# First q pieces on the ACT queue, and a split last eviction, in a two-layer attention kernel

## The chip, the cores and the metric

The kernel runs on one core of a Trainium2 chip. The metric is the device time of one execution in microseconds (us). The profile is that of one execution, taken by the hardware profiler. Engines are PE (matrix multiply), PEld (its weight loads, which overlap it), DVE, ACT, POOL and SP. SP computes nothing here: it issues the transfers (DMAs) between HBM and the on-chip memory SBUF. PE writes its results to PSUM, which has eight banks, and DVE or ACT copy them to SBUF ("eviction").

## The reference

```python
def _attn_ref(q, k, v):                      # batch 4, 12 heads, seq 448, head_dim 64
    scores = q @ k.T / sqrt(64), causal mask, softmax (eps 1e-9)
    return attn @ v
def _moe_ref(x, w_gate, wq, wk, wv, wo):     # x: 4 x 448 x 768, 4 experts, 2 chosen per token
    w = softmax over the two largest of x @ w_gate
    for e in range(4):                       # each expert is one causal attention head of width 64
        ye = causal_attention(x @ wq[e], x @ wk[e], x @ wv[e]) @ wo[e]
        out += (token chose e) * w_e * ye
    return out                               # 4 x 448 x 768
```

The output of the first layer, with its heads side by side, is the `x` of the second.

## The kernel before

The first layer works on 24 pairs of heads (four batches of six). A pair's k and q come as one tile `raw` of 128 partitions (two heads of 64) by 2 by 448 floats; index 0 of the middle dimension is k, index 1 is q. For each pair PE makes the scores in four row blocks (L362, in the order 1, 0, 2, 3), DVE subtracts the mask and takes the row maximum (L371), ACT takes the exponential (L378), POOL or ACT scales by the inverse sum, PE transposes (L407), DVE or ACT evicts, and PE multiplies with v (L422). The second layer of a batch projects x to queries and keys (L491) and to values and gates (L528), runs the same attention for two pairs of experts, and multiplies by `wo` in `output` (L594).

Nothing runs in the order in which it is written. Each step is put on record by `add(rank, kind, {engine: cost}, emit, after, bufs)`, and a planner (`Plan.run`) goes through an estimated time in which PE, ACT, DVE, POOL and "DMA" each do one step at a time: the ready step of the lowest rank starts. After that loop has ended, the line `for _, op, e in order: op.emit(e)` calls the recorded functions, in the order of their planned starts, and this writes the instructions of all queues. A step becomes ready 0.22 us after one on PE that it needs, and 0.2 us after one on another compute engine (FROM_PE, FROM_REST). The framework below adds the semaphores that the data need; each engine and each issuing queue then runs its instructions strictly in order.

The very first pair is loaded in four pieces (L449 to L454): the rows of k and q for columns 0 to 223, then those for columns 224 to 447, each 128 rows of 896 bytes, all issued by SP. Score blocks 1 and 0 need the first two pieces, blocks 2 and 3 all four. SP goes on with v of that pair (L470) and with whole tiles of the next pairs (L461).

`output(rank, b)` has a loop over m = 0 to 5, the 128-row parts of the output of batch b. Each has a PSUM bank (kind "pj", at most three at once; banks go back to a stock of eight and the one longest free is taken next). In the last batch the PE work of an m is two steps of three matmuls: pair 0, then pair 1. Then an eviction "ob" of 128x448 (ACT 0.43 or DVE 0.54 by the planner) goes into a half of the SBUF tile `ob`, and a store "st" (1.2 by the planner) from SP writes 128 rows of 1792 bytes to `out[b, m]` in HBM. In the other batches one store takes two m.

Of the kernel before, what the change touches and what calls it, by code (L numbers as in the profile page):

```python
# [17 lines left out]
def f32(ap):  # L18
    return ap.bitcast(F32)
# [24 lines left out]
class Plan:  # L44
# [16 lines left out]
    def add(self, rank, kind, on, emit, after=(), bufs=()):  # L61
        op = Op(rank, kind, on, emit, after, bufs)
        op.n = len(self.ops)
        self.ops.append(op)
        return op
# [122 lines left out]
def tile_attention_then_moe_attention(  # L188
# [27 lines left out]
    nc = tc.nc  # L216
    B, NM, _, S = out.shape
    NP = v.shape[1]
    P = 128
# [4 lines left out]
    DM = NM * P  # L224
# [64 lines left out]
    add = plan.add  # L289
# [9 lines left out]
    MOVE = {"ACT": 0.43, "DVE": 0.54}  # L299

    def copy(e, out, in_):
        if e == "ACT":
            nc.scalar.activation(out, in_, AF.Copy)  # L303
        else:
            nc.vector.tensor_copy(out, in_)  # L305
# [7 lines left out]
    def sub(e, out, a, b):  # L313
        eng = nc.gpsimd if e == "POOL" else nc.vector
        eng.tensor_tensor(out=out, in0=a, in1=b, op=ALU.subtract)  # L315
# [122 lines left out]
    def first_layer(b, p):  # L438
        rank = float(b * NP + p)
        raw, vt, hb, lb = Buf("raw"), Buf("v"), Buf("hi"), Buf("lo")  # L440
        first = (b, p) == pairs[0]
        full = b * NP + p in FULL
        cuts = (0, 2 * C, S) if first else (0, S)
        ready = []
        vl = None
        for lo, hi in zip(cuts, cuts[1:]):
            at = slice(lo, hi)
            part = (hi - lo) / S
            if first:  # L449
                loads = [  # L450
                    add(rank - 2.5, "ld", {"DMA": 0.6},
                        lambda e, n=n, at=at: nc.sync.dma_start(raw.at[:, n, at], qk[b, p, :, n, at]), (), [raw])
                    for n in range(2)
                ]  # L454
                hs = loads if full else [
                    add(rank + 0, "hi", {("DVE", "ACT")[n]: 0.32},
                        lambda e, n=n, at=at: copy(e, hb.at[:, n, at], raw.at[:, n, at]), [loads[n]], [raw, hb])
                    for n in range(2)
                ]
            else:  # L460
                loads = [add(rank - 2.5, "ld", {"DMA": 2.4}, lambda e: nc.sync.dma_start(raw.at, qk[b, p]), (), [raw])]  # L461
                hs = 2 * loads if full else 2 * [add(rank + 0, "hi", {"ACT": 0.85, "DVE": 0.54}, lambda e: copy(e, hb.at, raw.at), loads, [raw, hb])]
            ready += hs
            ready += hs if full else [
                add(rank - 1.5, "lo", {"POOL": 1.1 * part},
                    lambda e, n=n, at=at: sub(e, lb.at[:, n, at], raw.at[:, n, at], f32(hb.at)[:, n, at]), [hs[n]],
                    [raw, hb, lb])
                for n in range(2)
            ]
        vl = add(rank - 1.5, "ld", {"DMA": 1.2}, lambda e: nc.sync.dma_start(vt.at, v[b, p]), (), [vt])  # L470
        dest = xbuf[b, p] = Buf("x")
        xdone[b, p] = attention(
            rank, "a", b, p, [raw] if full else [hb, lb], ready, lambda h, j: vt.at[:, h * NC + j], [vl, vt], None, dest
        )

    def second_layer(b):
# [32 lines left out]
        for p in range(2):  # L509
# [3 lines left out]
                lambda h, j, p=p: vb.at[:, j, 2 * p + h], [vdone, vb], (gt, gdone), dest,  # L513
            )
        output(rank + 4, b)

    def values(rank, b, vb, gt, big):
# [63 lines left out]
    def output(rank, b):  # L581
        for m in range(DM // P):
            cols = slice(m * P, m * P + P)
            ps = Buf("pj")
            prev = None
            if m % 2 == 0:
                ob = Buf("osb")
                moved = []
            for ks in ((0,), (1,)) if b == B - 1 else ((0, 1),):

                def mm(e, ks=ks, ps=ps, cols=cols):
                    for p in ks:
                        for n, (w, t) in enumerate(((woh, 0), (woh, 1), (wol, 0))):
                            nc.tensor.matmul(  # L594
                                ps.at[:, :S], w[:, p, cols], ubuf[b, p].at[:, t],
                                start=(p == 0 and n == 0), stop=(p == 1 and n == 2),
                            )

                after = [udone[b, p] for p in ks] + [split[6 + p] for p in ks] + [prev]
                prev = add(rank, "pjo", {"PE": 0.62 * len(ks)}, mm, after, [ps] + [ubuf[b, p] for p in ks])  # L600
            moved.append(add(
                rank, "ob", MOVE,
                lambda e, m=m, ps=ps, ob=ob: copy(e, ob.at[:, m % 2], ps.at[:, :S]), [prev], [ps, ob],
            ))
            if b == B - 1:
                add(rank, "st", {"DMA": 1.2}, lambda e, m=m, ob=ob: nc.sync.dma_start(out[b, m], ob.at[:, m % 2]),
                    moved[-1:], [ob])
            elif m % 2:
                add(rank, "st", {"DMA": 2.4},
                    lambda e, m=m, ob=ob: nc.sync.dma_start(  # L610
                        out[b, m - 1:m + 1].rearrange("m p s -> p m s"), ob.at), moved, [ob])
# [18 lines left out]
    for b, p in pairs:  # L630
        first_layer(b, p)
# [43 lines left out]
```

## Time and profile before

| what | us |
|---|---|
| median of three runs | 331.93 |
| the runs | 331.35, 331.93, 1099.09 |
| the profiled execution | 331.19 |
| its span, first to last instruction | 329.4 |
| PE busy in it | 320.3 (97%) |
| ACT, DVE, POOL busy | 238.3, 214.7, 160.7 |
| DMA queue of SP, share of 16 DMA engines | 24.0% |

The span is what the views of the trace show; 1.8 us of the execution lie outside it. A busy share is a mean over stages that differ, so the views by stage are read beside it. A timeline row gives the start, the length, the engine, the source line, the operation, the tiles written and read, and in brackets the idle time before it with what ended it.

### The profile page before, as it was taken

Reading aid. Unit: us, or ns where it says so; the run is one execution under the profiler, and the core shown is the slowest. Engines: PE = TensorE matmul, PEld = TensorE weight load, DVE = VectorE, ACT = ScalarE, POOL = GpSimd, SP = SyncE. Lnnn points to the kernel's source line nnn. Section 1 sums busy time; section 2 is a strip of 40 time slices with the busy share of each in tenths; the row PEclk is TensorE's granted clock in tenths of the full one; section 3 lists DMA queues with packets and bytes.
Section 4 is the critical chain, followed back from the end, with each engine's and each line's share of the span. In section 5 each row is a group of like instructions: output and inputs, shape, how many; then the busy total and the mean of one; then the engine's idle time right before and its main releaser. Section 6 shows DMA issues by size and latency. Waiting matters only on the chain.

```text
span 329.4 us, 7473 instructions
## 1 busy us (share of the span) xinstructions
PE 320.3 (97%) x2584; PEld 259.5 (79%) x2584; DVE 214.7 (65%) x785; ACT 238.3 (72%) x743; POOL 160.7 (49%) x273
## 2 busy tenths in 40 slices
PE   5899999999999999999999999999999999999995
PEld 3467677778968977879799778887799978988784
DVE  2889789879688596466854599727672464544730
ACT  4999797779887699576875699948694464616833
POOL 2586989888985425909454136917421102001100
PEclk9999999999999999999999999999999999999999
DMA  5762563443362000163120010121000000000124
GB/s 167 248 192 87 158 201 125 132 111 100 103 194 90 2 30 29 57 203 135 56 63 22 2 50 10 30 102 67 2 2 3 0 0 2 1 2 0 58 111 167
DMA packets 11461, 25.65 MB, mean 78 GB/s; under 512 B 1184, under 2 KB 4768, under 8 KB 11424
## 3 DMA queue, kind: packets, MB, share of 16 engines
q1 hardware_dynamic: 11424, 25.18, 24.0%
q8 instruction: 20, 0.33, 0.4%
q14 instruction: 17, 0.14, 0.1%
HBM read 19.67 MB, written 5.51 MB: 76 GB/s over the span
## 4 chain that ended last, share of the span: by engine, by line
PE 62%; POOL 0%; ACT 0%; issue 0%
PE ps L491 14%; PE ps L422 12%; PE ps L407 11%; PE ps L594 9%; PE ps L362 9%; PE ps L528 8%; POOL five L311 0%; ACT raw L303 0%
## 5 line engine op out<-in xcount | busy, mean ns | idle before, releaser
L311 POOL TENSOR_SCALAR five<-five,stat 112x112 f32<-112x112 f32 (+3 forms) x218 | 105.5, 505 | 105.4 <-DVE stat L389 65.4
L378 ACT ACTIVATE five<-five,stat 112x336 f32<-112x336 f32 (+3 forms) x256 | 131.8, 518 | 14.6 <-DVE stat L371 14.5
L371 DVE CUSTOM_DVE_ANT_0 five<-ps,mask 112x224 f32<-112x224 f32 (+3 forms) x256 | 99.0, 442 | 31.1 <-PE ps L362 30.4
L407 PE MATMUL ps<-ident,five 112*112 112x112 f32 x640 | 70.6, 261 | 1.0 <-POOL five L311 0.5
L407 PEld LDWEIGHTS ps<-ident,five 112*112 112x112 f32 x640 | 63.4, 133 | 8.3 <-POOL five L311 2.2
L315 POOL TENSOR_TENSOR two<-raw,two 128x448 fp32r<-128x448 f32 x34 | 38.6, 1153 | 43.4 <-DVE two L305 10.7
L491 PE MATMUL ps<-two,wqkh 128*128 128x448 f32 x192 | 57.0, 377 | 0.4 <-DVE two L315 0.2
L303 ACT ACTIVATE five<-ps 112x448 f32<-112x448 f32 x92 | 46.5, 540 | 11.7 <-PE ps L407 11.0
L305 DVE COPY five<-ps 112x448 f32<-112x448 f32 x68 | 40.9, 620 | 20.7 <-PE ps L407 19.5
L422 PE MATMUL ps<-five,v 112*64 112x448 f32 (+3 forms) x384 | 50.3, 404 | 0.0
L378 ACT ACTIVATION_READ_ACCUMULATOR five<-five,stat 112x1 f32 x256 | 48.5, 189 | 0.0
L422 PEld LDWEIGHTS ps<-five,v 112*64 112x64 f32 x384 | 25.4, 137 | 23.6 <-issue 11.8
L362 PE MATMUL ps<-two,two 64*112 64x448 f32 (+3 forms) x400 | 41.7, 299 | 0.0
L491 PEld LDWEIGHTS ps<-two,wqkh 128*128 128x128 f32 x192 | 34.3, 188 | 4.4 <-issue 0.8
L315 DVE TENSOR_TENSOR two<-ps,two 128x448 fp32r<-128x448 f32 x48 | 29.9, 622 | 11.8 <-ACT two L303 10.8
L528 PE MATMUL ps<-wvh,two 128*112 128x260 f32 x192 | 35.7, 287 | 0.0
L491 PE MATMUL ps<-two,wqkl 128*128 128x448 f32 x96 | 35.1, 366 | 0.0
L362 PE MATMUL ps<-two 64*112 64x224 f32 (+3 forms) x200 | 33.3, 326 | 0.0
L362 PEld LDWEIGHTS ps<-two,two 64*112 64x112 f32 x400 | 31.4, 172 | 1.1 <-issue 0.2
L303 ACT ACTIVATE two<-ps 128x448 fp32r<-128x448 f32 x23 | 12.5, 543 | 24.4 <-PE ps L491 16.3
L528 PEld LDWEIGHTS ps<-wvh,two 128*112 128x112 f32 x192 | 28.0, 175 | 1.1 <-DVE stat L371 0.6
L594 PE MATMUL ps<-two,woh 128*128 128x448 f32 x96 | 28.1, 374 | 0.0
(55 smaller groups left out, 322.2 us busy)
## 6 DMA issues: line engine op xcount, KB each, us to landing
raw<-in_qk_dram SPq DMA_DIRECT2D x23, 448.0 KB, 3.6
v<-in_v_dram SPq DMA_DIRECT2D x24, 224.0 KB, 2.6
out_dram<-raw SPq DMA_DIRECT2D x9, 448.0 KB, 2.6
raw<-in_wqk_dram SPq DMA_DIRECT2D x4, 384.0 KB, 3.5
out_dram<-raw SPq DMA_DIRECT2D x6, 224.0 KB, 1.9
raw<-in_wvg_dram SPq DMA_DIRECT2D x2, 390.0 KB, 3.2
raw<-in_wo_dram SPq DMA_DIRECT2D x2, 384.0 KB, 3.0
raw<-in_qk_dram SPq DMA_DIRECT2D x4, 112.0 KB, 2.2
```

The costliest lines, as they stand in the source:

```text
L303: nc.scalar.activation(out, in_, AF.Copy)
L305: nc.vector.tensor_copy(out, in_)
L311: (nc.gpsimd if e == "POOL" else nc.vector).tensor_scalar(t, t, r, 1.0, op0=ALU.mult, op1=ALU.mult)
L315: eng.tensor_tensor(out=out, in0=a, in1=b, op=ALU.subtract)
L362: nc.tensor.matmul(banks[h].at[:C, :m], ops[x].at[sides[h], 1, qc], ops[y].at[sides[h], 0, :m], start=(n == 0), stop=(n == len(terms) - 1),)
L371: lambda e, h=h, i=i, m=m, bank=banks[h]: nc.vector.tensor_tensor_reduce(out=w(h, i), in0=bank.at[:C, :m], in1=mask[:, S - m:], scale=-0.1 ...
L378: lambda e, h=h, i=i: nc.scalar.activation(w(h, i), w(h, i), AF.Exp, bias=stat.at[:, 0, h, i:i + 1], scale=-1.0, accum_out=stat.at[:, 1, h ...
L407: nc.tensor.transpose(bank.at[:C, at * C:at * C + C], w(h, i)[:, j * C:j * C + C], ident[:C, :C])
L422: nc.tensor.matmul(acc.at[sides[h], j * C:S], vals(h, j), pt.at[:, bank, at:at + S - j * C], start=(j == 0), stop=(j == NC - 1),)
L491: nc.tensor.matmul(ps.at[:, :S], w[:, 2 * sel + p, k], xbuf[b, k].at[:, t], start=(k == 0 and n == 0), stop=(k == NP - 1 and n == 2),)
L528: nc.tensor.matmul(ps.at[:C, :VC], xbuf[b, k].at[:, t, c * C:c * C + C], w[:, k], start=(k == 0 and n == 0), stop=(k == NP - 1 and n == 2),)
L594: nc.tensor.matmul(ps.at[:, :S], w[:, p, cols], ubuf[b, p].at[:, t], start=(p == 0 and n == 0), stop=(p == 1 and n == 2),)
```

## The change

Two edits. In `first_layer`, the two q pieces of the first pair are issued by ACT, the two k pieces still by SP. In `output`, the eviction step gets a function `move`: where the flag `last` is true, ACT copies columns 0 to 223 and issues a store of them, and DVE copies columns 224 to 447 and SP issues a store of those; where it is false, the chosen engine copies all 448 columns. For the last m of the last batch the step is planned on ACT alone, and its store step is not added.

```diff
-                        lambda e, n=n, at=at: nc.sync.dma_start(raw.at[:, n, at], qk[b, p, :, n, at]), (), [raw])
+                        lambda e, n=n, at=at: (nc.sync, nc.scalar)[n].dma_start(raw.at[:, n, at], qk[b, p, :, n, at]), (), [raw])
...
-            moved.append(add(
-                rank, "ob", MOVE,
-                lambda e, m=m, ps=ps, ob=ob: copy(e, ob.at[:, m % 2], ps.at[:, :S]), [prev], [ps, ob],
-            ))
-            if b == B - 1:
+            last = b == B - 1 and m == DM // P - 1
+
+            def move(e, m=m, ps=ps, ob=ob):
+                for x, n in (("ACT", 0), ("DVE", 1)) if last else ((e, slice(None)),):
+                    n = slice(n * S // 2, (n + 1) * S // 2) if last else n
+                    copy(x, ob.at[:, m % 2, n], ps.at[:, :S][:, n])
+                    if last:
+                        (nc.scalar if x == "ACT" else nc.sync).dma_start(out[b, m, :, n], ob.at[:, m % 2, n])
+
+            moved.append(add(rank, "ob", {"ACT": 0.43} if last else MOVE, move, [prev], [ps, ob]))
+            if last:
+                pass
+            elif b == B - 1:
                 add(rank, "st", {"DMA": 1.2}, lambda e, m=m, ob=ob: nc.sync.dma_start(out[b, m], ob.at[:, m % 2]),
                     moved[-1:], [ob])
```

## Rows read from the trace of the kernel before

**Rows 1.** Busy time by stage, core 0, us from the start; columns as the head says.
```profile
core 0: us, PE busy (x) PEld busy (x) DVE busy (x) ACT busy (x) POOL busy (x), PEclk, DMA share, GB/s
0.00:3.50 3.50, 0.00 (x0) 0.00 (x0) 0.00 (x0) 1.28 (x1) 2.22 (x13) 1.00 0.43 104
3.50:5.40 1.90, 1.46 (x8) 1.16 (x8) 0.60 (x3) 0.17 (x1) 0.00 (x0) 1.00 0.92 234
5.40:12.00 6.60, 5.76 (x26) 3.06 (x26) 4.56 (x28) 6.05 (x24) 1.33 (x4) 1.00 0.61 195
12.00:20.00 8.00, 7.66 (x54) 4.65 (x56) 7.77 (x40) 7.97 (x29) 6.30 (x13) 1.00 0.69 229
20.00:100.00 80.00, 79.64 (x708) 61.45 (x705) 68.18 (x235) 68.81 (x225) 69.81 (x103) 1.00 0.47 141
100.00:300.00 200.00, 199.94 (x1622) 167.85 (x1621) 122.92 (x457) 138.90 (x430) 79.41 (x139) 1.00 0.12 38
```

**Rows 2.** The chain of waits, its end: start, length, what.
```profile
318.41 7.42 PE ps L594 x36
325.83 0.02 issue
325.86 0.54 ACT raw L303
```

**Rows 3.** Timeline, the first 6 us.
```profile
0.79 1.28 ACT L378 ACT_TABLE_LOAD   x1 [0.79 <-PEq L664]
0.80 1.80 SPq L452 DMA_DIRECT2D raw<-in_qk_dram  x4
2.64 0.43 SPq L470 DMA_DIRECT2D v<-in_v_dram  x1
3.58 1.46 PE L362 MATMUL ps<-raw 64*112 64x224 f32 x8 [3.58 <-DMA raw<-in_qk_dram]
...
5.23 0.48 ACT L378 ACTIVATE five<-five,stat 112x224 f32<-112x224 f32 x1 [3.15 <-DVE stat L371]
...
5.43 3.12 PE L362 MATMUL ps<-raw 64*112 64x336 f32 x14 [0.39 <-DMA raw<-in_qk_dram]
```

**Rows 4.** Line 452, the four piece loads: issue ns, then landing us (min/median/max).
```profile
L452 SPq DMA_DIRECT2D raw<-in_qk_dram x4: 372/422/432, 0.8 to 2.2; - x4
DMA to landing us min/median/max: 2.0/2.2/3.1
```

**Rows 5.** Two stretches: piece loads of 896-byte rows, stores of 1792-byte rows.
```profile
2.40:2.90 0.50, 0.00 (x0) 0.00 (x0) 0.00 (x0) 0.00 (x0) 0.50 (x4) 1.00 0.92 224
322.60:323.90 1.30, 1.30 (x9) 1.21 (x8) 0.00 (x0) 0.64 (x2) 0.00 (x0) 1.00 1.02 376
```

**Rows 6.** Timeline, the last evictions and stores.
```profile
321.05 1.74 ACT L303 ACTIVATE raw<-ps 128x448 f32<-128x448 f32 x3 [2.05 <-PE ps L594]
...
321.62 5.14 SPq L606 DMA_DIRECT2D out_dram<-raw  x6
...
323.45 0.54 ACT L303 ACTIVATE raw<-ps 128x448 f32<-128x448 f32 x1 [0.66 <-PE ps L594]
...
324.65 0.54 ACT L303 ACTIVATE raw<-ps 128x448 f32<-128x448 f32 x1 [0.66 <-PE ps L594]
...
325.86 0.54 ACT L303 ACTIVATE raw<-ps 128x448 f32<-128x448 f32 x1 [0.66 <-PE ps L594]
```

**Rows 7.** The sixth and last store's issue; then line 606, issue ns and landing us.
```profile
326.43 0.33 SPq L606 DMA_DIRECT2D out_dram<-raw  x1
...
L606 SPq DMA_DIRECT2D out_dram<-raw x6: 332/332/350, 321.6 to 326.4; - x6
...
DMA to landing us min/median/max: 1.9/1.9/2.0
```

**Rows 8.** DMA from 318 to 330 us in 40 slices of 0.3 us: GB/s.
```profile
GB/s 382 382 376 257 0 0 0 0 0 0 0 0 0 0 42 364 364 370 364 371 376 42 42 370 347 6 42 370 347 6 42 370 341 12 0 0 0 0 0 0
```

**Rows 9.** Copies out of PSUM by shape: busy us, mean ns of one, idle before.
```profile
L303 ACT ACTIVATE raw<-ps 128x448 f32<-128x448 f32 x20 | 10.9, 544 | 12.0 <-PE ps L594 11.6 <-issue 0.3
L305 DVE COPY vb<-ps 112x256 f32<-112x256 f32 x8 | 3.3, 423 | 4.0 <-PE ps L528 2.5 <-PE ps L422 1.3
L303 ACT ACTIVATE vb<-ps 112x256 f32<-112x256 f32 x8 | 3.1, 384 | 14.8 <-PE ps L528 10.9 <-PE ps L422 3.9
L305 DVE COPY raw<-ps 128x448 f32<-128x448 f32 x4 | 2.5, 624 | 2.3 <-POOL two L315 1.3 <-PE ps L594 0.9
```

**Rows 10.** Timelines of ACT and DVE: two copies of one PSUM bank.
```profile
248.04 0.39 ACT L303 ACTIVATE vb<-ps 112x256 f32<-112x256 f32 x1 [0.99 <-PE ps L528]
...
248.46 0.16 DVE L305 COPY gate<-ps 112x4 f32<-112x4 f32 x1 [2.07 <-ACT vb L303]
```

## Prediction

> **What bounds the kernel.** I read the busy time by stage first. From 20 us on, PE is busy 79.64 of 80 us and then 199.94 of 200 [rows 1]: no other engine's speed counts there. What PE does not fill lies at the two ends, and both edits are there. At the start PE waits 3.58 us for the first k and q pieces and 0.39 us more, at 5.43, for the other two [rows 3]; between 5.4 and 20 us it loses 0.84 and 0.34 us to ACT and DVE, ACT being busy 7.97 of 8 us [rows 1]. These follow the first scores, so what PE gains before 5.43 moves the rest with it. At the end the chain of waits reads PE until 325.83, one 0.54 us eviction on ACT, the end [rows 2]; then the last store is issued at 326.43 and lands 1.9 us later, at 328.33 [rows 7], 1.07 us before the span ends.
>
> **What the second edit really does.** The function `move` takes `m`, `ps` and `ob` as default arguments, but reads `last` from the loop around it. It is called when the planner has finished, long after the loop over m; by then `last` holds the value of m = 5. For batches 0 to 2 that is false, for the last batch it is true for all six m. The `if last: pass` branch, however, runs inside the loop and drops the store step of m = 5 only. So all six evictions of the last batch are split and store two halves each, and m = 0 to 4 are stored again whole. The stores go from 6 to 17, their bytes from 6 to 11 units of 229,376 B (224 KB), and five DRAM blocks are written twice.
>
> **Costs at the start.** SP issues a piece in 372 to 432 ns [rows 4], so q's first piece leaves at about 1.23 now and at 0.80 when ACT issues it. ACT is free: its only early work is the table load at 0.79, which carries the line of the first exponential, stands behind the two issues in its queue and, ending near 2.9, still precedes the first exponential at 5.23 [rows 3]. No row has a DMA issued by ACT; I price it as SP's, 0.33 to 0.43 us [rows 4, 7]. The gain is at most 0.43 us by issue. By transport: two pieces, 229,376 B, at the 224 GB/s of [rows 5] take 1.02 us, which is 0.51 more than one; the first piece, issued at 0.80, lands at 2.80 [rows 3, 4], so both by about 3.3, 0.3 before PE's 3.55. The 0.39 us wait for the second pieces is governed by one that takes 3.1 us to land [rows 4]; it is issued some 0.95 us earlier, but v and the next tile leave SP 0.9 us earlier too and compete. If it lands no sooner, PE gains nothing at all; if sooner, up to 0.4 + 0.39. A longer issue on ACT could cost 0.3. I take a gain of 0.35, range +0.8 to -0.3.
>
> **Costs at the end.** PE's own work is unchanged, 325.83 still (less the gain): banks are read until at most 323.35 for m = 2 below, while m = 5 starts at 324.65, so no matmul waits for a bank.
>
> A half copy on ACT: from 384 ns at 256 columns and 544 at 448 [rows 9], 0.83 ns a column, hence 0.36 us. On DVE, 423 and 624 give 0.39 us. The halves do not run together: a DVE copy of four columns from a bank that ACT reads sits idle 2.07 us and starts 0.03 us after ACT's copy ends [rows 10]. That both only read, and different columns, is what the Trainium skill ("PSUM — Partial Sum Buffer", section "PSUM bank collisions raise a hardware error") adds: two engines may not be in one bank of the same partitions at once, reads included. Side by side a split would be done 0.39 us after PE, in sequence after 0.78; that is 0.24 later than the 0.54 of now, with the row deciding.
>
> For m = 0 then: ACT 321.05 to 321.41, its store issued at 321.43, DVE to 321.83, SP's half store h0 at 321.86. ACT's issue holds up its next copy until 321.81 (m = 1 is ready at 321.65 [rows 6]); h1 follows at 322.61. Behind DVE nothing is queued. What matters is SP. A whole store f0 writes bytes that two half stores in flight are writing; I expect it to be held until these have landed, and everything behind it in SP's queue with it. The order is that of planned starts: counted from PE's end of m = 0, the evictions start at 0.22, 0.84, 1.46, 2.70, 3.94, 5.18, the whole stores at 0.85 (0.22 + 0.43 + 0.2) and then 1.2 apart. So SP has h0 h1 f0 h2 f1 h3 f2 h4 f3 h5 f4. The chain runs over every second one: h0 issued at 321.86, landing 2.0 us later as the smallest piece load [rows 4] (1.9 for a whole store [rows 7] is the other price), f0, then h2 0.34 later; h2 lands, f2, h4; h4 lands, f4 at 328.6, down at 330.5. That is 321.86 + 3 x 2.0 + 2 x 0.36 + 1.9, or 2.2 us after 328.33; with 1.9 each, 1.9 us.
>
> The second limit is the DMA engines. The stores alone run at 376 GB/s with rows of 1792 B, engines full [rows 5]. Half rows have 896 B, and the only stretch with such rows moved 224 GB/s at 0.92 busy. By that row six units of halves take 6.14 us and five whole ones 3.05; from the first data at 322.28 (0.85 us after an issue [rows 7, 8]) that ends at 331.47, landing 331.9: +3.6 us. At 376 GB/s for everything it is 6.7 us, landing 329.4: +1.1, and the chain above decides. The Trainium skill ("DMA: Bandwidth & Descriptors", section "Specifications") puts the row length for full rate at 512 B or more; by it the halves would lose nothing and the end would come at +2.2, but the row has 224 against 376. Part of the 224 may be SP's pace, though: a piece of 114,688 B every 0.43 us is 267 GB/s. Between 1.9 and 3.6 I take +2.7: slow halves also stretch the landings in the chain.
>
> Sum: -0.35 + 2.7 = +2.35 us, 333.5 for an execution like the profiled one (331.19). The two ordinary runs, 331.35 and 331.93, lie 0.2 and 0.7 above it; from their middle, 331.64, I predict **334.0 us**, 0.7% over.
>
> **Rivals.** (1) *The flag is seen per m*, as the diff reads: only m = 5 is split. Its DVE half is done at 326.64 and its store 0.24 us later than now; on 331.64 with -0.35 at the start, 331.5. Against it: the order of calls in the planner. (2) *Nothing holds the whole stores.* They go out as soon as SP is free, and the DMA engines alone decide: +1.1 to +3.6, on 331.64 less 0.35, 332.4 to 334.9. For it: no store of before waits for another (six are issued within 5.14 us [rows 6], each landing after 1.9), though none of those overlap. (3) *Slower by over 2%:* each whole store stands directly behind its own half in SP's queue. A link is then 2.0 + 0.36 us, five of them follow h0: h5 at 333.7, down at 335.7, +7.3; with landings of 2.2 us under load, +8.5; on 331.64 less 0.35, 338.6 to 339.8. It decides when the planned start of the next eviction (0.84) falls behind the store's (0.85) at every m; the planner's own spacing, 1.24 us for PE against 1.2 for stores, speaks against it. (4) *The start gets worse*, ACT's issue being slow: main case with +0.3 instead of -0.35, 334.6.
>
> **How the numbers follow.** Main case 0.70, rival 1 0.04, 2 0.15, 3 0.04, 4 0.07. Main case's own range: start -0.8 to 0, end +1.9 to +4.0 (0.4 for landings stretched on top of 3.6), on 331.2 to 331.9: 332.3 to 335.9. Rivals 2 and 4 lie inside. The range 332.0 to 336.2 leaves out rivals 1 and 3 and the tails. A change of 2% (6.6 us) is about what can be told from none: slower 0.05 (rival 3), faster 0.01, within 0.94.
>
> **What would show it.** In the new profile: 17 stores from the last batch instead of 6, twelve of 112 KB, and all six evictions as 128x224 copies on ACT and DVE; DVE's half starting after ACT's; whole stores of line `st` issued about 2 us after their halves, with SP waiting for DMAs; PE's last matmul 0 to 0.8 us earlier; the last landing 4 to 6 us after it, where it was 2.5. Wrong it is if one split eviction appears, if SP waits for no DMA, or if half stores move at 370 GB/s.

## The result

The changed kernel takes 334.37 us (median of four runs, 333.97 to 334.49) against 331.75 before: the ratio is 1.0087, 95% interval 1.0074 to 1.0100, some 2.9 us slower. The 331.75 still counts the run of 1099.09, which the ratio leaves out; without it the median is 331.58. 334.0 was predicted, in 332.0 to 336.2. The profiled execution took 333.97, its span is 332.2.

The stores of the last batch first. Here is SP's queue in the changed kernel, as a timeline (start us, length, line; L608 is a half store, L614 a whole one):

```profile
321.63 1.19 SPq L608 DMA_DIRECT2D out_dram<-raw  x2
323.45 0.33 SPq L614 DMA_DIRECT2D out_dram<-raw  x1
323.88 0.38 SPq L608 DMA_DIRECT2D out_dram<-raw  x1
324.36 0.40 SPq L614 DMA_DIRECT2D out_dram<-raw  x1
324.81 0.44 SPq L608 DMA_DIRECT2D out_dram<-raw  x1
326.19 0.33 SPq L614 DMA_DIRECT2D out_dram<-raw  x1
326.62 0.40 SPq L608 DMA_DIRECT2D out_dram<-raw  x1
327.70 0.33 SPq L614 DMA_DIRECT2D out_dram<-raw  x1
328.08 0.42 SPq L608 DMA_DIRECT2D out_dram<-raw  x1
329.26 0.33 SPq L614 DMA_DIRECT2D out_dram<-raw  x1
```

That is h0 h1 f0 h2 f1 h3 f2 h4 f3 h5 f4 in the prediction's names, eleven issues; the six of ACT come on top, so 17. The last one is f4, the whole store of m = 4, at 329.26, where the last of six was at 326.43 [rows 7]. The waits of SP over that stretch (who waited for whom: us, times, longest) name the reason, against none for a DMA among its stores before:

```profile
SPq L608 <- DVE raw L305: 5.6, 4, 4.4
SPq L614 <- DMA out_dram<-raw: 2.6, 4, 0.9
```

Some of that waiting is booked on semaphore instructions of line 614 in SP's queue (how many, then ns min/median/max):

```profile
L614 SPq EVENT_SEMAPHORE  x6: 17/28/675, 322.9 to 328.6; - x6
```

Those of the stores before took 17 ns each, and in e6 below they take a median of 1472 ns. So what holds a whole store is a semaphore wait that the framework put ahead of it in SP's queue, because its bytes overlap those of two earlier stores. What the transfers themselves would do without that wait, no run here shows.

The last evictions, in the same timeline, are the counterpart of [rows 6]:

```profile
325.63 0.36 ACT L303 ACTIVATE raw<-ps 128x224 f32<-128x224 f32 x1 [0.85 <-PE ps L594]
...
326.02 0.39 DVE L305 COPY raw<-ps 128x224 f32<-128x224 f32 x1 [0.81 <-ACT raw L303]
```

DVE begins when ACT is done, as in [rows 10]. And the start, the counterpart of [rows 3] and of the stage rows [rows 1]:

```profile
0.80 0.89 ACTq L452 DMA_DIRECT2D raw<-in_qk_dram  x2
...
0.80 0.86 SPq L452 DMA_DIRECT2D raw<-in_qk_dram  x2
...
1.72 1.28 ACT L378 ACT_TABLE_LOAD   x1 [1.72 <-PEq L672]
...
3.59 1.47 PE L362 MATMUL ps<-raw 64*112 64x224 f32 x8 [3.59 <-DMA raw<-in_qk_dram]
...
5.28 0.91 PE L362 MATMUL ps<-raw 64*112 64x336 f32 x2 [0.23 <-DVE stat L371]
```

```profile
20.00:100.00 80.00, 79.63 (x708) 61.55 (x705) 68.16 (x233) 68.76 (x225) 69.98 (x103) 1.00 0.47 141
100.00:300.00 200.00, 199.93 (x1623) 167.89 (x1622) 122.86 (x457) 138.75 (x429) 79.25 (x139) 1.00 0.12 38
```

q's pieces leave at 0.80 and the table load moves behind them, yet the first scores start at 3.59, where they started at 3.58. PE is as full from 20 to 300 us as it was, and its last matmul is evicted 0.23 us earlier (325.63 for 325.86), which is within the scatter of the profiles in the table below. The whole loss lies behind it.

### The profile page after: what moved, and what is told of

Read it like the earlier page. It is cut to its first block, busy times and chain, and to the rows that moved or that the text cites. A ratio compares the mean times of both kernels' runs of the same rounds, so it can differ in the third digit from the quotient of the medians.

```text
span 332.2 us, 7500 instructions
## 1 busy us (share of the span) xinstructions
PE 320.0 (96%) x2584; PEld 259.0 (78%) x2584; DVE 217.2 (65%) x791; ACT 237.1 (71%) x743; POOL 160.7 (48%) x273
## 4 chain that ended last, share of the span: by engine, by line
PE 93%; DVE 2%; ACT 1%; DMA 1%; POOL 1%; issue 0%; DVEq 0%
PE ps L407 19%; PE ps L422 19%; PE ps L362 18%; PE ps L491 18%; PE ps L528 11%; PE ps L594 9%; DVE two L305 1%; DMA raw<-in_qk_dram 1%; ACT five L378 1%; DVE five L371 1%; POOL five L311 1%; DVE two L315 0%; DVE raw L305 0%; ACT raw L303 0%; DVE stat L371 0%
```

## The experiments

The time up to the last eviction varies from one execution to the next: by 0.5 us (325.63 to 326.11) over the eight profiles that have both q pieces on ACT and the old choice of banks. So the tail is best read within each profile, from the start of the last eviction to the end of the span. The ratios are those to the kernel before, run on the same chip. Times alone compare less well: beside the runs below the kernel before has medians of 331.36 (e1 to e4), 331.32 (e5 to e8) and 331.56 us (e9 to e12), where most expectations were counted from 331.7.

| kernel | ratio (95% interval) | last eviction | span | tail |
|---|---|---|---|---|
| before | 1 | 325.86 | 329.4 | 3.5 |
| changed | 1.0087 (1.0074 to 1.0100) | 325.63 | 332.2 | 6.6 |
| e1 flag bound | 1.0027 (1.0017 to 1.0038) | 325.91 | 330.1 | 4.2 |
| e2 q on ACT only | 0.9994 (0.9985 to 1.0003) | 326.08 | 329.6 | 3.5 |
| e3 tail edit only | 1.0091 (1.0078 to 1.0105) | 325.87 | 332.4 | 6.5 |
| e4 no whole stores | 0.9992 (0.9983 to 1.0001) | 325.85 | 329.2 | 3.4 |
| e5 whole stores elsewhere | 1.0069 (1.0056 to 1.0082) | 326.05 | 331.9 | 5.9 |
| e6 whole store next | 1.0229 (1.0215 to 1.0243) | 325.80 | 336.9 | 11.1 |
| e7 new banks, q on ACT | 0.9965 (0.9951 to 0.9978) | 325.15 | 328.7 | 3.6 |
| e8 second q piece on ACT | 1.0002 (0.9992 to 1.0013) | 326.39 | 329.9 | 3.5 |
| e9 small whole stores | 1.0039 (1.0026 to 1.0051) | 326.11 | 331.2 | 5.1 |
| e10 new banks only | 0.9971 (0.9961 to 0.9981) | 325.72 | 329.2 | 3.5 |
| e11 new banks, no whole | 0.9956 (0.9942 to 0.9970) | 325.31 | 328.7 | 3.4 |
| e12 flag bound, order | 0.9995 (0.9986 to 1.0003) | 326.11 | 329.6 | 3.5 |

**e1, the flag bound.** The edit as its diff reads.

```diff
-            def move(e, m=m, ps=ps, ob=ob):
+            def move(e, m=m, ps=ps, ob=ob, last=last):
```

Expected: 

> The changed kernel with the flag bound when the function is made, so that only m = 5 of the last batch is split. Theory (whole stores held by their halves cost the 2.8 us): no byte is written twice, so nearly all of it goes; PE ends 0.22 earlier as in the changed kernel, DVE's half is done near 326.4, and m = 4's whole store, behind it in SP's queue, is issued near 326.8 and lands near 328.8: +0.4 on 331.7, so 332.0 to 332.2. Rival (the split in sequence is what costs): still most of it, 333.5 or more.

332.1 us: two thirds of the loss go, on the theory's side. What is left, 0.9 us by the ratio, is seen in SP's queue, where m = 4's whole store stands behind m = 5's half, which waits for DVE:

```profile
326.71 0.33 SPq L608 DMA_DIRECT2D out_dram<-raw  x1
327.14 0.41 SPq L614 DMA_DIRECT2D out_dram<-raw  x1
```

**e12, the flag bound and that order changed.** The planner is told a shorter store, and puts m = 4's store first.

```diff
-            def move(e, m=m, ps=ps, ob=ob):
+            def move(e, m=m, ps=ps, ob=ob, last=last):
...
-                add(rank, "st", {"DMA": 1.2},
+                add(rank, "st", {"DMA": 0.6},
```

Expected: 

> The changed kernel with the flag bound, and the stores of the last batch planned at 0.6 instead of 1.2, so that m = 4's store stands before m = 5's half in SP's queue. Theory (the 0.9 us of the run with the flag bound are that store's place): the last landing is that of DVE's half, 326.4 + 1.7 = 328.2 or so: 331.2 to 331.5, level with the kernel before. Rival (the split in sequence costs): 332.0.

331.39, ratio 0.9995: the 0.9 us were the order, as SP's queue shows, with all five whole stores ahead of the half.

```profile
321.88 3.93 SPq L614 DMA_DIRECT2D out_dram<-raw  x5
326.92 0.33 SPq L608 DMA_DIRECT2D out_dram<-raw  x1
```

What the edit set out to do is worth nothing either way: the tail is 3.5 us with one copy of 0.54 us and one store, and with two copies in sequence and two stores. The half store lands in 1.7 us, the whole one in 1.9 to 2.0, which pays for the later copy.

**e2 and e8, the start.** e2 takes the first edit alone; e8 puts only q's second piece on ACT.

```diff
-  nc.sync.dma_start(raw.at[:, n, at], qk[b, p, :, n, at])
+  (nc.sync, nc.scalar)[n].dma_start(raw.at[:, n, at], qk[b, p, :, n, at])                       # e2
+  (nc.scalar if n and at.start else nc.sync).dma_start(raw.at[:, n, at], qk[b, p, :, n, at])    # e8
```

Expected of e2: 

> The start edit alone. Theory (the first two pieces are bound by transport, so only the second wait shrinks): first scores at 3.55 to 3.60 as before, second group at 5.28, PE ends 0.2 earlier, 331.5 (-0.2). Rival (the issue time counts): first scores 0.3 to 0.4 earlier, 331.2.

Expected of e8: 

> The kernel before with q's second piece alone on ACT. Theory (the first pieces are bound by transport, and the gain is that of the second pieces): the same as the start edit, second group at 5.28, 331.5. Rival (q's first piece on ACT matters): no gain, 331.7; should the second pieces take transport from the first, first scores later than 3.6.

Neither is told from no change: 1 lies inside both intervals. Of what was expected of e2, first scores at 3.58 and the second group at 5.27 are there, but PE does not end sooner (last eviction at 326.08). In e8 first scores start at 3.80, the sign that its expectation named for second pieces that take transport from the first, though in one profile only; in the other profiles with both q pieces on ACT they start between 3.29 and 3.59, in those with all on SP at 3.58, 3.49 (e3) and 3.44 (e10). These scatter by 0.3 us among like programs, so at 0.43 us the edit's gain in issue is hard to see in any one profile. The busy time of two early stretches, before and then changed, shows what the transfers do meanwhile:

```profile
1.75:2.25 0.50, 0.00 (x0) 0.00 (x0) 0.00 (x0) 0.33 (x1) 0.40 (x3) 1.00 0.61 165
2.25:3.50 1.25, 0.00 (x0) 0.00 (x0) 0.00 (x0) 0.00 (x0) 0.73 (x4) 1.00 0.95 225
```

```profile
1.75:2.25 0.50, 0.00 (x0) 0.00 (x0) 0.00 (x0) 0.50 (x1) 0.41 (x3) 1.00 0.70 93
2.25:3.50 1.25, 0.00 (x0) 0.00 (x0) 0.00 (x0) 0.75 (x1) 0.73 (x4) 1.00 1.07 324
```

With two queues the first half microsecond moves less here (93 GB/s for 165) and the rest more (324 for 225). If the rate is taken as even over the second stretch, as many bytes as two pieces have, 229,376, are in by 2.8 to 2.9 us either way: 0.5 x 165 + 0.65 x 225 is 229 kB at 2.90, 0.5 x 93 + 0.57 x 324 is 231 kB at 2.82. The second pieces do come sooner: no profile with both q pieces on ACT waits for a DMA at the second group, while before and e10 do (e3 does not). But behind that wait stands another, for DVE to read a bank, at 5.28. Nor is a sooner start seen at the end: in e4 and e6 first scores start at 3.29, and their last evictions, at 325.85 and 325.80, lie among those of the six like profiles that start at 3.52 to 3.59 (325.63 to 326.11).

**e3, the tail edit alone.** The changed kernel with line 452 as it was.

```diff
-  (nc.sync, nc.scalar)[n].dma_start(raw.at[:, n, at], qk[b, p, :, n, at])
+  nc.sync.dma_start(raw.at[:, n, at], qk[b, p, :, n, at])
```

Expected: 

> The tail edit alone, as delivered, all pieces on SP. Theory: the whole of the loss is here, 331.7 + 2.8 = 334.5 to 334.6, 0.2 over the changed kernel. Rival (the second queue at the start slows later transfers): at most half of it, 333.

334.24, ratio 1.0091: the whole loss is the second edit's.

**e4, no whole stores.** Six split evictions and twelve half stores remain.

```diff
-            if last:
+            if b == B - 1:
                 pass
```

Expected: 

> The changed kernel without the five whole stores: six split evictions, twelve half stores, each byte written once. Theory: nothing is held; DVE's last half is done near 326.4 and its store lands 1.8 to 2.0 later, 331.5 to 331.8. Rival (halves are slow to move, 224 GB/s): 12 halves take 6.1 us from 322.0, landing 328.6 or later, and with slow sequence 332.2 or more.

331.04, and a tail of 3.4 us, no longer than before. So neither the split in sequence nor the width of the halves costs anything: they land in 1.7 to 1.8 us (line 608 of this kernel, its landings):

```profile
DMA to landing us min/median/max: 1.7/1.7/1.8
```

While they move, the DMA engines are 0.76 busy at 246 GB/s (busy time of a stretch of this kernel; last two columns):

```profile
322.30:327.80 5.50, 3.51 (x18) 2.95 (x16) 1.93 (x5) 1.43 (x4) 0.00 (x0) 1.00 0.76 246
```

**e5, whole stores elsewhere, and e9, whole stores cut down.** These two take the five whole stores apart. e5 writes them to a scratch tensor in DRAM that nothing reads: all the bytes, no bytes written twice. e9 stores only 16 of 128 rows of them: the same waits, 0.14 MB instead of 1.15.

```diff
-  nc.sync.dma_start(out[b, m], ob.at[:, m % 2])
+  nc.sync.dma_start(scratch[m], ob.at[:, m % 2])              # e5
+  nc.sync.dma_start(out[b, m, :16], ob.at[:16, m % 2])        # e9
```

Expected of e5: 

> The changed kernel with the five whole stores of the last batch written to another DRAM tensor that nothing reads: the same bytes and the same number of transfers, but no byte is written twice, so no store has to wait for another of the same bytes. Theory (the waits cost, not the bytes): 2.52 MB at some 345 GB/s from 322.0 end near 329.3 and land near 329.8, 1.4 before the changed kernel: 332.9. Rival (the DMA engines alone decide): as the changed kernel, 334.3.

Expected of e9: 

> The changed kernel with the five whole stores cut to 16 of 128 rows: the same transfers, waits and queue order, but 0.14 MB written twice instead of 1.15. Theory (after the run with the second copies in another tensor, 2.3 of the 2.9 us are the extra bytes): only the chain of waits with unloaded landings is left, 321.63 + 3 x 1.7 + 2 x 0.36 and a last landing of 1.7, 329.2, 0.9 to 1.1 over the kernel before: 332.2 to 332.5. Rival (the waits are the cost, whatever the bytes): 334.0 or more.

e5 takes 333.58, between the 332.9 of my theory and the 334.3 of its rival. By the ratio it is 2.3 us over the kernel before, where the theory had 1.2 and the rival 2.6 over 331.7: so nearer to the rival. e9 takes 333.01, 1.3 over by the ratio, where 0.9 to 1.1 was expected. In e5 SP waits for no DMA before a store, and the DMA engines are the limit, 0.98 busy at 333 GB/s (busy time of a stretch; the last two columns), with whole stores that land in 2.3 to 3.4 us:

```profile
322.60:329.80 7.20, 3.42 (x18) 2.85 (x16) 1.84 (x5) 1.43 (x4) 0.00 (x0) 0.93 0.98 333
```

```profile
L615 SPq DMA_DIRECT2D scratch_dram<-raw x5: 404/538/582, 323.3 to 328.0; - x5
...
DMA to landing us min/median/max: 2.3/2.9/3.4
```

In e9 the engines have gaps (0.68 busy at 211 GB/s in the same stretch) and the same chain of waits sets the end, with h2 issued at 324.36 and h4 at 326.72; SP, timeline:

```profile
322.11 1.19 SPq L608 DMA_DIRECT2D out_dram<-raw  x2
323.94 0.33 SPq L614 DMA_DIRECT2D out_dram<-raw  x1
...
326.30 0.33 SPq L614 DMA_DIRECT2D out_dram<-raw  x1
...
328.63 0.33 SPq L614 DMA_DIRECT2D out_dram<-raw  x1
```

Each limit stands by itself: 2.3 us for the bytes, 1.3 for the waits. Together they make 2.9 rather than 3.6. I take this to be because the waits fall largely into time in which the engines are busy anyway: in the stretch above they are 0.89 busy in the changed kernel. No run takes the overlap apart.

**e6, each whole store directly behind its halves.** The prediction's third rival, made real.

```diff
+                if last and m < DM // P - 1:
+                    nc.sync.dma_start(out[b, m], ob.at[:, m % 2])      # at the end of move
...
-            if last:
+            if b == B - 1:
                 pass
```

Expected: 

> The changed kernel with each whole store issued directly behind its own halves, so that SP's queue reads h0 f0 h1 f1 and so on. Theory (every link is one landing): five links of 2.0 to 2.3 + 0.36 us behind 321.63 put h5 at 333.4 to 334.9 and its landing at 335.4 to 336.9, 4.2 to 5.7 over the changed kernel: 338.5 to 340. Rival (the DMA engines alone decide): no change, 334.3.

338.81, ratio 1.0229: the same 17 stores and bytes, 4.7 us more than in the changed kernel by the two ratios, by order alone. SP's timeline has five links of 2.3 to 2.7 us, from one half store (L608) to the next, with the whole store of the same m (L610) in between:

```profile
321.80 0.35 SPq L608 DMA_DIRECT2D out_dram<-raw  x1
323.63 0.35 SPq L610 DMA_DIRECT2D out_dram<-raw  x1
324.08 0.39 SPq L608 DMA_DIRECT2D out_dram<-raw  x1
326.34 0.33 SPq L610 DMA_DIRECT2D out_dram<-raw  x1
326.73 0.42 SPq L608 DMA_DIRECT2D out_dram<-raw  x1
328.86 0.33 SPq L610 DMA_DIRECT2D out_dram<-raw  x1
329.29 0.39 SPq L608 DMA_DIRECT2D out_dram<-raw  x1
331.23 0.33 SPq L610 DMA_DIRECT2D out_dram<-raw  x1
331.61 0.42 SPq L608 DMA_DIRECT2D out_dram<-raw  x1
333.58 0.33 SPq L610 DMA_DIRECT2D out_dram<-raw  x1
334.00 0.38 SPq L608 DMA_DIRECT2D out_dram<-raw  x1
```

**e7, e10 and e11, new banks.** The wait for DVE at 5.28 came from the program: in the built program the first eight score matmuls write the banks called 82, 83, 85, 86 and then 82, 89, 83, 85, since a freed bank is taken before a new one is made. e7 makes new ones up to eight, with q on ACT; e10 does that alone; e11 adds it to e4.

```diff
-  b.at = stock[home].pop(0) if stock[home] else make(home)
+  new = home == "ps" and make.n[home] < 8
+  b.at = stock[home].pop(0) if stock[home] and not new else make(home)
```

Expected of e7: 

> The start edit with the output of before, and PSUM banks taken new until all eight are in use, so that the first score blocks do not wait for DVE to read a bank. Theory: the second group of scores starts when the first ends, 5.06, 0.37 before the kernel before: 331.3. Rival (ACT, busy without a gap from 12 to 20 us, sets the pace there): nothing beyond the start edit alone, 331.5.

Expected of e10: 

> The kernel before with new PSUM banks until eight are in use, all pieces on SP. Theory (the 1.2 us of the run with both came from the banks, the ACT queue being worth nothing): 330.1 to 330.3. Rival (the second pieces, landing late from SP, now set the second group's start): 331.0 or more.

Expected of e11: 

> New banks, q on ACT, and six split evictions with each byte stored once. Theory (twelve half stores cost nothing and end up to 0.2 earlier): 329.8 to 330.1, the best so far or level with it. Rival (with other banks the evictions hold a matmul): 330.5.

All three are faster than the kernel before: 330.0, 330.57 and 330.34, by 0.3 to 0.4%, and 1 lies outside all three intervals. In e7 the scores of the first pair run without a gap, from 3.56 to 7.64:

```profile
3.56 4.08 PE L363 MATMUL ps<-raw 64*112 64x224 f32 x16 [3.56 <-DMA raw<-in_qk_dram]
```

In e10, where SP loads all pieces, the wait for DMA is back, and it is 0.48 us:

```profile
5.38 0.90 PE L363 MATMUL ps<-raw 64*112 64x336 f32 x2 [0.48 <-DMA raw<-in_qk_dram]
```

So in this execution the wait that e10's rival named is there, and yet the median of e10 is below the rival's 331.0. But the profiled execution was e10's slowest (331.19 of 330.33 to 331.19), so it doesn't show the gain, nor whether the others have that wait. By which step the banks help is therefore left open: e7 gains 1.2 us by its ratio, and the second group's sooner start had been priced at 0.37. That q on ACT adds to the banks isn't settled either, nor that e11's split does: the three intervals overlap. e11 lies between its theory (329.8 to 330.1) and its rival (330.5); what the rival names is not seen, for PE runs its last 36 matmuls without a gap, from 317.87 to 325.29.

## Why the prediction was right

**The flag.** Shown: the late reading of `last` splits all six evictions and doubles five stores, and binding it takes two thirds of the loss away (e1). Rival 1 put such a kernel 0.1 us under the kernel before; it is 0.9 over: I had missed that the half of m = 5 then stands ahead of m = 4's whole store in SP's queue, though I had written down that very order (e12).

**The order in SP's queue and the hold.** Shown, store by store, as a semaphore wait on SP. The chain was right and its links were too short in sum: 2.0 us was taken for each landing, and from the issue of a half to that of its whole store there are 1.8 (h0 to f0), 2.3 (h2 to f2) and 2.6 us (h4 to f4). That the loaded engines stretch them is borne out by e9, where they are 1.8, 1.9 and 1.9 us. f4 was put at 328.6 with PE's end where it was; it came at 329.26 with PE 0.23 earlier, so 0.9 late on that scale.

**The DMA engines.** Right as a limit, wrong in its price. Half rows are not held to 224 GB/s: in e4 they move 246 GB/s with engines that are only 0.76 busy, and cost nothing there, and halves and wholes mixed move at 333 GB/s in e5. Nor are halves alone seen at the 370 GB/s that the prediction named as a sign of being wrong: that stretch of e4 has 246. The upper bound of 3.6 us was therefore too high; the engines alone make 2.3. The Trainium skill's line of 512 bytes ("DMA: Bandwidth & Descriptors", section "Specifications") lies nearer to e5 (333 GB/s, where whole rows alone had 376 [rows 5]) than the row that I weighed against it. That row was of one queue at the beginning of the program; with two, the changed kernel moves 324 GB/s soon after, half rows and the transfers behind them together.

**The sum at the end.** +2.7 was taken between 1.9 and 3.6. The tail grew from 3.5 to 6.6 us in the profiles, +3.0, and e3 has 3.0 by its ratio. That 2.7 came so near is in part luck: it was chosen between two bounds of which the upper was mispriced. Neither limit alone gives the loss, and rival 2 (no hold, engines alone) is not what happens, though e5 shows that it would have cost 2.3 of the 2.9 us.

**The start.** This term was probably too large: 0.35 us was taken, and the edit alone gives 0.9994 (0.9985 to 1.0003), 0.2 us, at most 0.5 and perhaps nothing. By transport I had the two pieces at 3.3, and only the two profiles that move the most in the first half microsecond come that early; the slower first half microsecond of most profiles with two queues seems to give the gain back. That what PE gains before 5.43 moves the rest with it isn't seen either: e4 and e6 started 0.3 us sooner and did not end sooner than the others. And I had not looked at what stands behind the wait at 5.43: DVE's read of a bank that the second group reuses, which lets go only 0.15 us before 5.43.

**The halves in sequence.** Shown: 0.36 and 0.39 us (0.36 and 0.39 forecast), DVE 0.03 us after ACT.

## What to carry to other kernels

When steps are recorded first and emitted later, read every loop variable in a recorded function as its last value unless it is bound; the profile's count of stores by line tells it at once. Bytes written twice cost more than transport: the framework has the second store wait on a semaphore until the first has landed, and everything behind it in that queue waits too; where it stands in the queue decided between 2.9 and 7.6 us here. Before speeding up one wait, look for the next one behind it: second pieces that were issued some 0.9 us sooner gained nothing that could be measured, with a bank behind them that was not yet free.

## What the runs showed of the hardware

SP takes longer to issue a store where the DMA engines are loaded: a median of 0.33 us in e4 (engines 0.76 busy), 0.54 (up to 0.58) for the whole stores of e5 (0.98 busy). The first half microsecond of transfers (1.75 to 2.25 us) is slow, and a second queue makes it uneven rather than faster: 147, 152 and 165 GB/s in the three profiles with all pieces on SP, 63 to 116 in seven of the ten with both q pieces on ACT, 152, 174 and 211 in the other three. The two with 174 and 211 are those in which the first scores start at 3.29.
